# Weight tiles of group 0 prepared in three steps instead of two, and one product moved ahead on VectorE

## Chip, cores and metric

One core of a Trainium2 chip runs the whole kernel. The metric is the device time of one execution in microseconds; before, the median of three runs is 947.73 us (946.85 to 948.97).

## What is computed

A linear-attention layer (4 batches, 8 heads, 768 positions, 48 channels a head) is followed by two feed-forward layers of 3072 tokens, 384 model channels and 2048 inner channels.

```python
def _attn_ref(r, k, v, w, u):
    for t in range(S):
        kt, vt, rt = (k[:, :, t], v[:, :, t], r[:, :, t])
        cur = np.einsum('bhd,bhe->bhde', u[None] * kt, vt)
        y[:, :, t] = np.einsum('bhd,bhde->bhe', rt, state + cur)
        state = w[None, :, :, None] * state + np.einsum('bhd,bhe->bhde', kt, vt)

def _moe_ref(x, w_in, w_out):
    h = x @ w_in
    return (h * (1.0 / (1.0 + np.exp(-1.702 * h)))) @ w_out

def _moe2_ref(x, w_in, w_out):
    h = x @ w_in
    sp = np.where(h > 20.0, h, np.log1p(np.exp(np.minimum(h, 20.0))))
    return (h * np.tanh(sp)) @ w_out
```

The weights of both feed-forward layers come as 64-bit floating-point numbers.

## The kernel before, in words

**Tokens and blocks.** The 3072 tokens are 24 blocks of 128 (`j`), and six groups of 512 (`g`). Attention works block by block; for the first four blocks (j = 0 to 3, the tokens of group 0) it runs alone, lines 694 to 729. From then on (line 779) each of the 16 steps of a group, one for each tile of 128 inner channels (`m`), does the feed-forward work of one tile, and the attention of one further block is spread over four steps: its phases are `ph` 0 (`unit_a`, the products of queries and keys, and the mask), 1 (`unit_kv`, `unit_y`), 2 (`unit_x`, the additions to the state T, the next block's `products` and `powers`, its loads) and then `values`, `early_bonus` and `diagonal` for the next block. Block 4 starts one step late.

**Precision by split operands.** Each operand of a feed-forward product is split into a high part, rounded for TensorE, and a low part, the rest. A product takes three matmuls for each 128 rows: high x high, low x high, high x low (`PASSES`). `product_in` (line 596) makes `h` with nine matmuls of 512 columns, `product_out` (line 742) adds nine to the three accumulators `acc`. Step m issues `product_in` of tile m and, near its end, `product_out` of tile m - 1.

**A weight tile's way** (class `Layer`, lines 56 to 172). A tile holds the 768 columns that one step needs. `fetch(m)` (line 74) is five transfers on SP's queue into a raw buffer (`rawa`); tiles share three of these in turn, so a fetch waits until the tile three before has been read. `bits(m, 0)`, `bits(m, 1)`, `bits(m, 2)` are three DVE instructions over 128 x 768 (lines 123, 129, 132), which take the 32-bit pattern out of the 64-bit numbers into a pattern buffer (`wva`). `high(m)` is one ACT copy of the pattern to the rounded high part (line 155). `low(m, half)` subtracts high from pattern for 384 columns (line 163): half 0 on POOL, half 1 on DVE in group 0, and both on POOL for tiles 0 and 1.

**Order in group 0.** Nothing plans the order: each engine works through its instructions in the order of the code. `BARE_TILES` (line 35) tiles, 0 and 1, are prepared during the four bare blocks: `bits(0)` and its parts in j = 1, `bits(1)` and its parts in j = 2 (lines 711 to 724). In step m of group 0 (lines 796 to 803 and 820) come, in this order, the high part of tile m + 1 (ACT), its low part (POOL, DVE), the fetch of tile m + 4 (SP), and the first two pattern instructions of tile m + 2 (DVE), then gelu (line 804) and `gh` (line 805) on ACT, `gl` on DVE (line 806), the attention work of phases 0 or 2, and the third pattern instruction of tile m + 2. (Step 0 has no high, low or fetch, as tile 1 is ready.) So on DVE a step is low part, two pattern instructions, `gl`, attention, the third pattern instruction; on ACT it is high part, gelu, `gh`.

**Phase 2 on DVE** (lines 810 to 814): the split of x (`unit_x`, line 522: ACT copies `y` to `xha`, DVE subtracts for `xla`, line 528), two additions to T (line 520, or copies, line 518), and `products(j + 1)` (line 385, written to a tile `Am`), which the small matmuls `pa` of `early_bonus` (line 393) need; ACT then makes eight diagonal tiles from it (line 419). In group 0 `products` runs in steps 3, 6 and 10 (blocks 5, 6 and 7).

**Buffers.** The pattern buffer of a tile is `x2_1` for odd and `x2_3` for even m (lines 621 and 622); both names, as `x2_0` and `x2_2`, later hold results of the first layer, which are written from group 1 on. From group 1 on all sixteen weight tiles stay in SBUF, and steps prepare none.

Of the kernel before, what the change touches and what calls it, by code (L numbers as in the profile page):

```python
# [25 lines left out]
NF = 16  # L26
# [5 lines left out]
W_LO, W_HI = 0.8, 1.25  # L32
R2 = math.sqrt(0.5)
RAW = 3
BARE_TILES = 2
LAG = 4
NB = 2

# [557 lines left out]
def product_in(nc, lay, m, x, n, pool, name):  # L596
    h = pool.tile([P, 512], F32, tag="h", name=name)
    k = 0
    for kt in range(3):
        for wz, xz in PASSES:  # L600
            nc.tensor.matmul(h[:, :n], lhsT=lay.win(m, wz, kt), rhs=x[xz][:, kt, :], start=k == 0, stop=k == 8)  # L601
            k += 1
    return h


def feed_forward(tc, ctx, ins, out, w_sb, chk, consts, general):
# [4 lines left out]
    V, A = nc.vector, nc.scalar  # L611

    wpool = ctx.enter_context(tc.tile_pool(name="wpool", bufs=NF))
    spool = ctx.enter_context(tc.tile_pool(name="spool", bufs=2))
    xpool = ctx.enter_context(tc.tile_pool(name="xpool", bufs=2))
    x2pool = ctx.enter_context(tc.tile_pool(name="x2pool", bufs=1))
# [2 lines left out]
    late = {}  # L619

    l1 = Layer(nc, w1, wpool, lambda m: (x2pool, "x2_2", 1) if m % 3 == 2 else (spool, "raw", 2),
               lambda m: (x2pool, "x2_1" if m % 2 else "x2_3", 1, 768), "a", chk, spool, general, True)
    l2 = Layer(nc, w2, wpool, lambda m: (late["x"], "x2_5", 1) if m % 3 == 1 else (spool, "raw", 2),
               lambda m: (late["x"], "wv", 2, 768) if m % 4 > 1 else (late["b"], "sy"[m % 4], 2, NB * 512), "b", chk, spool, general)
    x2, xs, xs2 = {}, {}, {}
# [1 line left out]
    def new_x(g, tag):  # L627
        n = GROUPS[g]
        return (xpool.tile([P, 3, n], F32R, tag="xh", name=f"xh{tag}{g}"),
                xpool.tile([P, 3, n], F32R, tag="xl", name=f"xl{tag}{g}"))  # L630
# [20 lines left out]
    at = Attention(nc, apool, cpool, psum, chan, tok, general)  # L651

    def unit_x(j):
        t = j * C
        g = max(z for z in range(NG) if starts[z] <= t)
        if g not in xs:
            xs[g] = new_x(g, "a")
        at.unit_x(j, xs[g], t - starts[g])
# [27 lines left out]
    def parts(m):  # L686
        l1.high(m)
        l1.low(m, 0)
        l1.low(m, 1)
# [4 lines left out]
    for j in range(n_bare):  # L694

        more = j + 2 < n_bare
        at.unit_y(j, "acc", 3)
        if more:
            at.products(j + 2)
            at.powers(j + 2, V)  # L700
        if j + 1 == n_bare:
            unit_x(j)
        elif not general:
            for z in range(2):
                at.mask(j + 1, z)
        at.unit_t(j, 0, V)
        at.unit_t(j, 1, V)
        at.values(j + 1, G)
        if j + 1 < n_bare:
            at.unit_kv(j + 1, "y", 1)  # L710
        if j == 1:
            l1.bits(0)
        if j + 1 < n_bare:
            unit_x(j)
        if more:
            at.early_bonus(j + 2, "acc", 3)
            at.diagonal(j + 2, 0)
            at.diagonal(j + 2, 1)
            at.unit_a(j + 2)
        if j == 1:  # L720
            parts(0)
        if j == 2:
            l1.bits(1)
            parts(1)
        if general or j:
            at.load_rk(j + NRK)
        at.load_tok(j + 2)
        if j < 3:
            l1.fetch(j + 2)
# [12 lines left out]
    def product_out(g, m, gt):  # L742
        n = GROUPS[g]
        if m == 0:
            acc[g] = [psum.tile([P, 512], F32, tag="acc", name=f"acc{g}_{z}", bufs=3) for z in range(3)]
        for ct in range(3):
            for k, (wz, gz) in enumerate(PASSES):
                nc.tensor.matmul(acc[g][ct][:, :n], lhsT=l1.wout(m, wz, ct), rhs=gt[gz],  # L748
                                 start=m == 0 and k == 0, stop=m == NF - 1 and k == 2,
                                 skip_group_check=True)  # L750

    def evacuate(g):
        n = GROUPS[g]
        x2[g] = (x2pool if g < NG - 2 else late["x"]).tile([P, 3, n], F32, tag=f"x2_{g}", name=f"x2_{g}")
        for ct in range(3):
            if ct == 0 or g == NG - 1 or (ct == 1 and g == NG - 2):
                A.activation(out=x2[g][:, ct, :], in_=acc[g][ct][:, :n], func=AF.Copy)
            else:
                V.tensor_copy(out=x2[g][:, ct, :], in_=acc[g][ct][:, :n])
# [3 lines left out]
    def range_check(n):  # L763

        if n >= len(checks):
            return
        if n == 0:
            l1.check(0, 0)
            l1.check(1, 0)
        lay, m, part = checks[n]  # L770
        lay.check(m, part)
        if part == 1 and 0 < n < len(checks) - 2:
            lay, m, part = checks[n + 2]
            lay.check(m, 0)

    pend = None
    d = BARE_TILES
    checked = 0
    for g in range(NG - 1):
        n = GROUPS[g]  # L780
        for m in range(NF):

            j, q = n_bare + (g * NF + m) // 4, m % 4
            on = j < NJ

            ph = q - 1 if j == n_bare else q
            h = product_in(nc, l1, m, xs[g], n, hpool, f"h{g}_{m}")
            e = d - 1 if d > BARE_TILES else NF
            if on and ph == 0:
                at.unit_a(j)  # L790
            if on and ph == 1:
                at.unit_kv(j)
                at.unit_y(j)
            gh = gpool.tile([P, n], F32R, tag="gh", name=f"gh{g}_{m}")
            gl = gpool.tile([P, n], F32R, tag="gl", name=f"gl{g}_{m}", bufs=1 if general else 2)
            if g == 0:

                l1.high(e)
                l1.low(e, 0)
                l1.low(e, 1, V)  # L800
                l1.fetch(e + RAW)
                l1.bits(d, 0)
                l1.bits(d, 1)
            A.activation(out=h[:, :n], in_=h[:, :n], func=AF.Gelu_apprx_sigmoid)  # L804
            A.activation(out=gh, in_=h[:, :n], func=AF.Copy)  # L805
            V.tensor_tensor(out=gl, in0=h[:, :n], in1=gh.bitcast(F32), op=ALU.subtract)  # L806
            if on and ph == 0 and not general:
                for z in range(2):
                    at.mask(j, z)
            if on and ph == 2:  # L810
                unit_x(j)
                at.unit_t(j, 1, V)
                at.bonus(j + 1, 2, V)
                at.products(j + 1)

            for _ in range(0 if g == 0 else 2 if m % 8 == 7 else 1):
                range_check(checked)
                checked += 1
            if g == 0:
                l1.bits(d, 2)  # L820
                d += 1
            if on and ph == 0:
                at.bonus(j + 1, 0, G)
            if on and ph == 1:
                at.unit_t(j, 0, V if g == 0 else G)
                at.bonus(j + 1, 1, G)
            if on and ph == 2:
                at.load_rk(j + NRK)
                at.load_tok(j + 2)
                at.powers(j + 1, V if g == 0 else G)  # L830
            if on and q == 3:
                at.values(j + 1, G)
            if pend is not None:
                product_out(*pend)
                if pend[1] == NF - 1:
                    evacuate(pend[0])
            if on and (q == 3 or ph < 0):
                i = j if ph < 0 else j + 1
                at.early_bonus(i, "A", 2)
                at.diagonal(i, 0)  # L840
                at.diagonal(i, 1)
            pend = (g, m, (gh, gl))
# [220 lines left out]
```

## Time and profile before

| | |
|---|---|
| median of three runs | 947.73 us (946.85 to 948.97) |
| profiled execution | 946.47 us, of which the span is 944.6 us |
| PE busy | 908.9 us (96%) |
| DVE busy | 496.1 us (53%) |
| ACT busy | 570.9 us (60%) |
| POOL busy | 182.3 us (19%) |

The span runs from the first to the last instruction of the execution that was profiled. Engines: PE is TensorE, DVE VectorE, ACT ScalarE, POOL GpSimd, SP the engine that issues most transfers. A row of the time line gives the start, the length, engine, line and operation, output and inputs, their shapes and the count; in square brackets stands how long the engine had been idle and what ended that. A matmul's name lists one of its inputs: `h<-xha,wa` has the high part of x, `h<-xla,wa` the low one; `acc<-gh,wa` and `acc<-gl,wa` likewise. Numbers of buffers are left out, so every tile's pattern is called `wva`. PEclk is the granted TensorE clock as a share of 2.4 GHz.

### The profile page before, as it was taken

How to read it: one execution, taken by the hardware profiler on the slowest of the kernel's cores; microseconds unless marked ns; L12 is line 12 of the kernel's file. 1: busy time of each engine (PE TensorE's matmuls, PEld its weight loads, DVE VectorE, ACT ScalarE, POOL GpSimd, SP SyncE). 2: the span in 40 equal slices, each digit the busy share in tenths (PEclk: the TensorE clock that was granted, in tenths of full speed). 3: DMA queues.
4: the chain of work that ended last, by engine and by line, in shares of the span. 5: the costliest groups of instructions: out<-in, count | busy, mean ns of one | idle time of the engine just before them, and what ended most of it. 6: DMA issues, size and time to landing. Idle time of an engine off the chain costs nothing.

```text
span 944.6 us, 14242 instructions
## 1 busy us (share of the span) xinstructions
PE 908.9 (96%) x5766; PEld 770.2 (82%) x5766; DVE 496.1 (53%) x690; ACT 570.9 (60%) x896; POOL 182.3 (19%) x171
## 2 busy tenths in 40 slices
PE   6679999999999999999999889999999999999997
PEld 5567778887877878788888778999999999999986
DVE  7788873223223223322499556565555555555653
ACT  4344445546565555663355667677777777777773
POOL 3313353222432223320034012001010010010000
PEclk9799999999999999999999999999999999999999
DMA  9675633444344364431255000000000000000001
GB/s 203 162 185 151 177 109 109 143 136 156 112 142 143 112 182 121 135 122 35 70 197 200 2 1 1 1 33 1 34 1 1 34 1 1 34 1 1 34 1 37
DMA packets 34907, 78.42 MB, mean 83 GB/s; under 512 B 4368, under 2 KB 23568, under 8 KB 34832
## 3 DMA queue, kind: packets, MB, share of 16 engines
q1 hardware_dynamic: 33952, 77.09, 28.0%
q8 instruction: 47, 0.77, 0.4%
q10 hardware_dynamic: 880, 0.33, 0.2%
q14 instruction: 28, 0.23, 0.1%
HBM read 72.68 MB, written 4.72 MB: 82 GB/s over the span
## 4 chain that ended last, share of the span: by engine, by line
PE 78%; DVE 11%; issue 5%; DMA 3%; POOL 1%; ACT 1%; SPq 1%; ACTq 0%; DVEq 0%; POOLq 0%
PE bcc L591 20%; PE k L601 20%; PE acc L748 16%; PE h L601 14%; PE y L500 3%; PE A L443 2%; DVE wvb L132 2%; DVE wvb L129 2%; DVE wva L123 1%; DMA rkbuf<-in_chan_dram 1%; DVE wva L132 1%; PE kv L480 1%; DVE wb L163 1%; DVE wvb L123 1%; DVE gl L882 1%
## 5 line engine op out<-in xcount | busy, mean ns | idle before, releaser
L591 PE MATMUL bcc<-wb,bh 128*128 128x384 f32 x768 | 211.5, 337 | 0.0
L601 PE MATMUL h<-xha,wa 128*128 128x512 f32 x576 | 183.0, 398 | 3.6 <-POOL wa L163 2.7
L601 PE MATMUL k<-xhb,wb 128*128 128x512 f32 x576 | 180.8, 395 | 4.5 <-DVE y L554 2.6
L748 PE MATMUL acc<-gh,wa 128*128 128x512 f32 x576 | 184.7, 402 | 0.0
L806 DVE TENSOR_TENSOR gl<-h,gh 128x512 fp32r<-128x512 f32 x80 | 55.3, 691 | 228.9 <-ACT gh L805 228.2
L591 PEld LDWEIGHTS bcc<-wb,bh 128*128 128x128 f32 x768 | 140.4, 188 | 4.1
L804 ACT ACTIVATE h<-h 128x512 f32<-128x512 f32 x80 | 46.5, 581 | 144.7 <-PE h L601 141.9
L601 PEld LDWEIGHTS h<-xha,wa 128*128 128x128 f32 x576 | 109.8, 191 | 29.4 <-POOL wa L163 4.0
L591 PE MATMUL bcc<-wb,bl 128*128 128x384 f32 x384 | 129.1, 336 | 0.9 <-DVE bl L578 0.9
L748 PEld LDWEIGHTS acc<-gh,wa 128*128 128x128 f32 x576 | 105.0, 188 | 27.8 <-issue 3.2
L601 PEld LDWEIGHTS k<-xhb,wb 128*128 128x128 f32 x576 | 107.1, 189 | 24.1 <-DVE y L554 3.4
L554 DVE TENSOR_TENSOR y<-k,s 128x512 f32<-128x512 f32 x96 | 66.2, 692 | 94.0 <-ACT s L553 89.7
L601 PE MATMUL k<-xlb,wb 128*128 128x512 f32 x288 | 114.4, 397 | 0.0
L601 PE MATMUL h<-xla,wa 128*128 128x512 f32 x288 | 113.9, 396 | 0.0
L748 PE MATMUL acc<-gl,wa 128*128 128x512 f32 x288 | 113.7, 395 | 0.1
L565 DVE SCALAR_TENSOR_TENSOR y<-s,y 128x1024 f32<-128x1024 f32 x48 | 59.9, 1249 | 83.1 <-ACT s L564 83.1
L553 ACT ACTIVATE s<-k 128x512 f32<-128x512 f32 x96 | 57.4, 599 | 65.0 <-PE k L601 64.4
L591 PEld LDWEIGHTS bcc<-wb,bl 128*128 128x128 f32 x384 | 72.1, 188 | 5.5 <-DVE bl L578 1.6
L563 ACT ACTIVATE s<-s,one 128x1024 f32<-128x1024 f32 x48 | 55.4, 1154 | 34.1 <-DVE y L554 34.1
L642 POOL TENSOR_TENSOR xlb<-x,xhb 128x512 fp32r<-128x512 f32 x18 | 24.7, 1376 | 264.4 <-DVE xhb L641 258.8
L601 PEld LDWEIGHTS h<-xla,wa 128*128 128x128 f32 x288 | 55.2, 192 | 12.3 <-DVE xla L528 0.3
L748 PEld LDWEIGHTS acc<-gl,wa 128*128 128x128 f32 x288 | 54.1, 188 | 13.3 <-DVE gl L882 0.5
(119 smaller groups left out, 1180.2 us busy)
## 6 DMA issues: line engine op xcount, KB each, us to landing
chka<-in_w_dram SPq DMA_DIRECT2D x16, 768.0 KB, 4.5
chkb<-in_w_dram SPq DMA_DIRECT2D x16, 768.0 KB, 4.4
rawb<-in_w_dram SPq DMA_DIRECT2D x16, 768.0 KB, 4.3
tkv<-in_tok_dram SPq DMA_DIRECT2D x24, 384.0 KB, 5.9
rkbuf<-in_chan_dram SPq DMA_DIRECT2D x46, 192.0 KB, 5.1
rawa<-in_w_dram SPq DMA_DIRECT2D x48, 96.0 KB, 2.6
rawa<-in_w_dram SPq DMA_DIRECT2D x16, 288.0 KB, 3.6
out_dram<-o SPq DMA_DIRECT2D x10, 384.0 KB, 3.1
```

The lines of the kernel that those rows point to most:

```text
L132: V.scalar_tensor_tensor(out=v, in0=L, scalar=29, in1=v, op0=ALU.logical_shift_right, op1=ALU.bitwise_or)
L500: self.nc.tensor.matmul(y[32 * s:32 * s + rows, C * x:C * x + C], lhsT=lhsT, rhs=rhs, start=n == 0, stop=n == len(jobs[s]) - 1, skip_group ...
L553: nc.scalar.activation(out=self.s[:, z, :n], in_=h[:, :n], func=AF.Sigmoid)
L554: nc.vector.tensor_tensor(out=self.y[:, z, :n], in0=h[:, :n], in1=self.s[:, z, :n], op=ALU.mult)
L563: nc.scalar.activation(out=s, in_=s, func=AF.Arctan, scale=-1.0, bias=self.one)
L565: nc.vector.scalar_tensor_tensor(out=y, in0=s, scalar=R2, in1=y, op0=ALU.add, op1=ALU.mult)
L591: self.nc.tensor.matmul(self.acc[g][t][:, :DM], lhsT=gt[gz][:, t * P:t * P + P], rhs=self.lay.wout(m, wz), start=m == 0 and k == 0, stop=m ...
L601: nc.tensor.matmul(h[:, :n], lhsT=lay.win(m, wz, kt), rhs=x[xz][:, kt, :], start=k == 0, stop=k == 8)
L642: nc.gpsimd.tensor_tensor(out=xl[:, z, :], in0=x2[g][:, z, :], in1=xh[:, z, :].bitcast(F32), op=ALU.subtract)
L748: nc.tensor.matmul(acc[g][ct][:, :n], lhsT=l1.wout(m, wz, ct), rhs=gt[gz], start=m == 0 and k == 0, stop=m == NF - 1 and k == 2, skip_grou ...
L804: A.activation(out=h[:, :n], in_=h[:, :n], func=AF.Gelu_apprx_sigmoid)
L806: V.tensor_tensor(out=gl, in0=h[:, :n], in1=gh.bitcast(F32), op=ALU.subtract)
```

## The change

A third pattern buffer is taken (`x2_0`), and three tiles are begun ahead of group 0: tile 0 is ready, tile 1 has its high part from block j = 2 and gets both halves of its low part on POOL in j = 3, tile 2 gets its three pattern instructions in j = 3, ahead of that block's `unit_x`. In step m of group 0 the high part is now that of tile m + 2, the low part that of tile m + 1 (none in step 0), the fetch that of tile m + 5, and the pattern instructions those of tile m + 3. In phase 2 `products(j + 1)` is moved ahead of `unit_x` and the additions to T.

```diff
-BARE_TILES = 2
+BARE_TILES = 3
...
     l1 = Layer(nc, w1, wpool, lambda m: (x2pool, "x2_2", 1) if m % 3 == 2 else (spool, "raw", 2),
-               lambda m: (x2pool, "x2_1" if m % 2 else "x2_3", 1, 768), "a", chk, spool, general, True)
+               lambda m: (x2pool, ("x2_1", "x2_3", "x2_0")[m % 3], 1, 768), "a", chk, spool, general, True)
...
         if j + 1 == n_bare:
+            l1.low(1, 0)
+            l1.low(1, 1)
+            l1.bits(2)
             unit_x(j)
...
         if j == 2:
             l1.bits(1)
-            parts(1)
+            l1.high(1)
...
-            e = d - 1 if d > BARE_TILES else NF
...
             if g == 0:
 
-                l1.high(e)
-                l1.low(e, 0)
-                l1.low(e, 1, V)
-                l1.fetch(e + RAW)
+
+                l1.high(d - 1)
+                if m:
+                    l1.low(d - 2, 0)
+                    l1.low(d - 2, 1, V)
+                l1.fetch(d + RAW - 1)
                 l1.bits(d, 0)
                 l1.bits(d, 1)
...
             if on and ph == 2:
+                at.products(j + 1)
                 unit_x(j)
                 at.unit_t(j, 1, V)
                 at.bonus(j + 1, 2, V)
-                at.products(j + 1)
```

## Rows read from the trace of the kernel before

**Rows 1.** Busy time by stretch: PE, PEld, DVE, ACT, POOL; PEclk, DMA share, GB/s.

```profile
42.00:139.00 97.00, 88.38 (x626) 69.02 (x627) 83.20 (x106) 42.66 (x91) 33.28 (x29) 0.95 0.60 159
139.00:480.00 341.00, 341.00 (x2553) 273.59 (x2552) 108.35 (x182) 187.97 (x415) 89.32 (x84) 1.00 0.41 123
```

**Rows 2.** Waits of PE, 42 to 139 us: total us, times, longest us.

```profile
PE pa L393 <- DVE Am L385: 5.1, 2, 4.3
PE h L601 <- POOL wa L163: 2.7, 3, 1.5
...
PE kv L480 <- DVE Am L447: 0.5, 1, 0.5
```

**Rows 3.** Waits of all engines, 38 to 140 us.

```profile
DVE wa L163 <- ACT wa L155: 11.7, 12, 2.6
```

**Rows 4.** Time line of DVE, steps 2 and 3 of group 0.

```profile
54.98 0.95 DVE L132 SCALAR_TENSOR_TENSOR wva<-rawa,wva 128x768 int32<-128x768 int32 x1
56.84 0.56 DVE L163 TENSOR_TENSOR wa<-wva,wa 128x384 fp32r<-128x384 f32 x1 [0.91 <-ACT wa L155]
57.31 1.38 DVE L123 TENSOR_SCALAR wva<-rawa 128x768 int32<-128x768 int32 x1
...
59.60 0.69 DVE L806 TENSOR_TENSOR gl<-h,gh 128x512 fp32r<-128x512 f32 x1
60.20 0.95 DVE L132 SCALAR_TENSOR_TENSOR wva<-rawa,wva 128x768 int32<-128x768 int32 x1
...
62.07 0.56 DVE L163 TENSOR_TENSOR wa<-wva,wa 128x384 fp32r<-128x384 f32 x1 [0.45 <-ACT wa L155]
...
65.42 0.55 DVE L528 TENSOR_TENSOR xla<-y,xha 128x384 fp32r<-128x384 f32 x1
...
66.62 0.69 DVE L385 TENSOR_TENSOR Am<-rkbuf 112x512 f32<-112x512 f32 x1
```

**Rows 5.** Time line of ACT, step 2.

```profile
57.32 0.60 ACT L805 ACTIVATE gh<-h 128x512 fp32r<-128x512 f32 x1
```

**Rows 6.** Chain that ended last, end of group 0: start, us, work.

```profile
136.55 2.10 PE acc L748 x9
138.65 2.04 PE h L601 x9
```

**Rows 7.** Time line of PE, end of step 3 and first product of step 4.

```profile
67.46 1.02 PE L393 MATMUL pa<-ublk,Am 112*128 112x2 f32 x8 [4.26 <-DVE Am L385]
68.35 1.10 PE L601 MATMUL h<-xha,wa 128*128 128x512 f32 x2
...
72.17 1.16 PE L443 MATMUL A<-rkbuf 48*128 48x128 f32 x16
```

**Rows 8.** Time lines of DVE and POOL ahead of group 0.

```profile
38.27 0.96 DVE L132 SCALAR_TENSOR_TENSOR wva<-rawa,wva 128x768 int32<-128x768 int32 x1
41.90 0.56 DVE L528 TENSOR_TENSOR xla<-y,xha 128x384 fp32r<-128x384 f32 x1 [2.67 <-ACT xha L527]
...
40.18 1.95 POOL L163 TENSOR_TENSOR wa<-wva,wa 128x384 fp32r<-128x384 f32 x2 [2.76 <-ACT wa L155]
```

**Rows 9.** Time line of DVE, pattern instructions in step 0 and for tile 1.

```profile
36.60 1.63 DVE L129 SCALAR_TENSOR_TENSOR wva<-rawa,wva 128x768 int32<-128x768 int32 x1
...
46.35 0.55 DVE L123 TENSOR_SCALAR wva<-rawa 128x768 int32<-128x768 int32 x1
46.94 0.96 DVE L129 SCALAR_TENSOR_TENSOR wva<-rawa,wva 128x768 int32<-128x768 int32 x1
```

**Rows 10.** Time line of PE, first products of steps 8 and 12.

```profile
92.06 0.56 PE L601 MATMUL h<-xha,wa 128*128 128x512 f32 x1 [0.99 <-POOL wa L163]
...
95.54 1.26 PE L443 MATMUL A<-rkbuf 48*128 48x128 f32 x16
...
114.32 0.51 PE L601 MATMUL h<-xha,wa 128*128 128x512 f32 x1 [0.28 <-ACT wa L155]
116.37 0.79 PE L601 MATMUL h<-xha,wa 128*128 128x512 f32 x1 [1.55 <-POOL wa L163]
```

## The prediction

> **What bounds the kernel now.** I read the busy time of long stretches first [rows 1]. From 139 to 480 us TensorE is busy for all of its 341 us, so nothing done for another engine can help there. The stretch from 42 to 139 us is group 0 of the first layer: TensorE is busy 88.38 of 97 us, and its granted clock is 0.95 on the mean, so some products run at 1.2 instead of 2.4 GHz. The change touches group 0 and the 42 us ahead of it alone. What it saves there should reach the end undiminished, because TensorE works without a break behind it.
>
> Next, who lets TensorE wait in group 0 [rows 2]: the small bonus product `pa` waits 5.1 us for DVE's product of queries and keys (4.3 in one piece), and the first product `h` 2.7 us for POOL's part of a weight tile. In the list for all engines [rows 3] DVE's half of the low part waits 11.7 us, twelve times, for ACT's high part of the same tile.
>
> The time line of DVE in steps 2 and 3 shows why [rows 4]. DVE ends the last pattern instruction of a tile at 55.93 (54.98 + 0.95) and starts its half of that tile's low part only at 56.84: in these 0.91 us ACT makes the high part. From one third-pattern instruction (L132, 54.98) to the next (60.20) the loop takes 5.22 us. A step of TensorE, a product in and a product out, takes 2.04 + 2.10 = 4.14 us at full clock [rows 6]. So the loop through DVE and ACT, not TensorE, paces group 0, and TensorE pays where it catches up: for 4.26 us it has nothing until `pa` at 67.46, and the product behind it runs at 1.2 GHz [rows 7].
>
> **The change, part by part.** *Low part one step behind the high part.* In step m ACT now makes the high part of tile m+2, and POOL and DVE the low part of m+1, whose high part is a step old. No instruction is added to a step. DVE's wait goes: its loop becomes 5.22 - 0.91 = 4.31 us, an estimate that keeps every duration of rows 4. What is late next is `gl`, which needs ACT's `gh`: from 55.93 to the end of `gh` (57.32 + 0.60) it is 1.99 us [rows 5], and with `gl` (0.60 from its start to the next) and L132 (0.95) 3.54, less than 4.31. ACT's high part stays at the same place ahead of the gelu and waits for the same point of DVE, one tile on. Cost on ACT: nothing; if that cover were gone, a late pattern would hold the gelu back as it does now.
>
> *Fetches.* Each tile's five transfers still follow, on SP's queue, a pattern instruction three tiles earlier and lead their reader by the same number of steps; the `rk` and `tok` loads keep their places behind them. One fetch moves from step 1 to step 0. I cost them at nothing: in the list of waits no work on weights waits for a transfer. Were a lead too short, DVE would stop at L123.
>
> *Product behind `gl` (steps 3, 6 and 10).* In each of these steps the product passes the split of x and the two additions to T. In step 3 the product starts at 66.62, `xla` at 65.42 [rows 4], so it comes 1.20 us earlier. Those it passes start 0.6 us later; the split is read by group 1, the additions by a product three steps on, so this costs nothing unless their readers come up close behind.
>
> *Ahead of group 0.* Three pattern instructions for tile 2 now stand before the split of block 3, at a place where DVE idles from 39.23 to 41.90 [rows 8]. Alone they last 0.55 + 0.96 + 0.95 = 2.46 us (the first two as they run undisturbed in rows 9) and would fit; no delay is the lower end. But POOL makes its two halves of tile 1 there, 1.95 us from 40.18. The upper end: two held-up instructions, at 0.83 each (below), that is 39.23 + 2.46 + 1.66 = 43.35, or 1.4 us late. I take 0.9, beside the lower middle, since the first instruction ends before POOL starts. Step 1 gives the same 0.9 back by its own lost wait (one of the twelve), so the two cancel.
>
> *POOL beside DVE.* L123 takes 1.38 us with POOL's low part beside it [rows 4] and 0.55 alone [rows 9]: 0.83 us of DVE. The move lets POOL run a step earlier, so another instruction of DVE meets it. Bounds: a gain of 0.83 where it falls into a wait, a loss of 0.83 where it meets a second instruction. I take 0, as rows 4 hold one such meeting per step already. The Trainium skill, GPSIMD Engine Reference, section Specifications, speaks against the change here: POOL's SBUF interfaces are shared with VectorE, with contention for instructions in a 2-port mode or with two SBUF inputs. By that rule L129, L132 and the low part are all exposed, and a second meeting per step (14 x 0.83 = 11.6 us) would cost more than the sum below gives; the trace agrees as far as L123 and, at 1.63 us [rows 9], L129 go.
>
> **The sum.**
> - Step 3: `pa` starts earlier by 0.91 (step 2's wait) + 0.45 (step 3's own, the wait before 62.07 in rows 4) + 1.20 (order) = 2.56 us.
> - Step 4: the product at 1.2 GHz takes 72.17 - 68.35 = 3.82 instead of 2.04 us [rows 7, 6]. With the pause cut to about 1.7 us I take full clock: 1.78. If the clock still falls, 0.
> - Step 8: a pause of 0.99 for POOL's low part, and eight matmuls in 95.54 - 92.06 = 3.48 instead of 8/9 of 2.04 = 1.81 [rows 10]: 2.66.
> - Step 12: pauses of 0.28 and 1.55, and the eight matmuls behind them as in step 8, 1.67 [rows 10]: 3.50.
> - Step 15: a pause of 0.17, the third of rows 2's waits for POOL.
>
> Together 10.7 us. Against it stands that DVE's new loop (4.31) is still a little longer than TensorE's step (4.14): over the twelve steps in which patterns are made, 12 x 0.17 = 2.0 us of new short waits. Between nothing (waits filled by attention products) and 4 (attention work on DVE adds as much again) I take 2.0. Net 8.7 us. The profiled execution took 946.47 us (span 944.6 and 1.9 around it), hence 937.8; it lies 1.26 below the median of the runs shown (947.73), so I forecast **939.0**.
>
> **Rivals.**
> *DVE stays the pace (0.17).* POOL meets a second instruction of DVE in half of the 14 steps: 7 x 0.83 = 5.8 us, leaving 2.9: 944.8. For it: DVE is busy 83.20 of 97 us [rows 1]. Against: POOL's low parts are short, and DVE has instructions that read PSUM between.
>
> *The wait only moves (0.07).* DVE reaches `gl` 0.9 us sooner and waits there for `gh`, and the weights are late as before: 947.7. For it: ACT's chain is untouched. Against: the 3.54 us worked out above, and that the low part's inputs are a whole step old.
>
> *TensorE's clock falls more often (0.11), slower than before.* Today three products run at 1.2 GHz, each behind a pause of 1 to 4 us. If the long pauses become short ones in every step, the clock may stay low over several products, at 1.78 us each (3.82 against 2.04). The place is steps 1 to 12. From five products at 1.2 GHz beyond those cleared, the 8.7 us are used up; eight cost 14.2, giving 947.7 - 8.7 + 14.2 = 953.2. Against it: with 8.6 us of pauses the clock of group 0 was still 0.95 on the mean [rows 1], and the pause that I leave in, 0.5 us for the mask [rows 2], is shorter than any ahead of a slow product. The Trainium skill, TensorE: Matmul & The Clock Gate, section "A second HAM failure mode: psum-queue depth-cycling", says that frequent micro-idles between groups of matmuls make the clock oscillate; the trace shows that only behind the longer pauses.
>
> **How the numbers follow.** The forecast has 0.65, and 935.5 to 941.5 alone; its low end is with no new waits and a little more won of what there is: pauses of 5.1 + 2.7 + 0.5 + 0.3 = 8.6 us [rows 2, 10] and slow products of 1.78 + 2 x 1.67 = 5.1 are 13.7 together, which would give 934.0. The range 934.5 to 945.0 takes in most of the first rival and leaves out about 2 in 10. A measurement of this kernel can tell 0.2% (1.9 us) from no change. Faster by more: 0.65 + 0.17 = 0.82; within: 0.07; slower: 0.11.
>
> **What would show it.** Right: DVE's low part waits for ACT near 0 instead of 11.7 us; no wait of `h` for POOL; `pa`'s long wait under 2.5 us; the clock of 42 to 130 us at 0.98 or more; TensorE without a pause from about 130 us on, and all later stretches as long as before. Wrong: `gl` waiting for `gh`, L129 at 1.6 us throughout (first rival), a granted clock below 0.95 in group 0 (third), DVE stopped at L123 for a transfer, or the split of block 3 starting over 2 us later than 41.90.

## Result and profile after

The changed kernel takes **934.73 us** (median of four runs, 934.06 to 935.54) against 947.29 for the kernel before beside it: ratio 0.9874, 95% interval 0.9849 to 0.9898, 12.6 us faster. The forecast was 939.0, and the range began at 934.5. A second measurement of the same kernel, in a later group of runs, gave 936.17 us and a ratio of 0.9895 (0.9877 to 0.9913), 9.6 us. The gain is 10 to 13 us; the forecast of 8.7 was somewhat small, and two of the four runs of the first measurement lie just below the range. Two profiles of the changed kernel were taken, the first of a run of 934.06 us, the second, with the later group, of one of 936.45.

Busy time by stretch, the changed kernel, first profile (columns as in [rows 1]); group 0 now runs from 39.5 to 127.3 us:

```profile
42.00:128.00 86.00, 85.39 (x624) 68.54 (x623) 76.19 (x102) 42.18 (x90) 33.36 (x29) 0.95 0.68 176
128.00:467.00 339.00, 339.00 (x2544) 271.92 (x2543) 106.56 (x181) 186.58 (x413) 88.16 (x83) 1.00 0.40 124
```

TensorE is busy for all but 0.6 of 86 us, where it was idle for 8.6 of 97. The window begins just behind a pause of 0.78 us inside the first product, to which the section on the start of group 0 comes back. The list of waits of all engines (38 to 130 us) says who waits instead, the changed kernel first, then the kernel before (38 to 140 us):

```profile
...
ACT wa L155 <- DVE wva L132: 28.0, 11, 3.9
ACT h L808 <- PE h L601: 15.8, 9, 3.6
DVE gl L810 <- ACT gh L809: 9.0, 8, 2.8
...
PE h L601 <- DVE xla L528: 0.8, 1, 0.8
PE pa L393 <- DVE Am L385: 0.6, 1, 0.6
...
PE h L601 <- ACT xha L527: 0.6, 1, 0.6
```

```profile
...
ACT wa L155 <- DVE wva L132: 46.5, 14, 4.9
...
ACT h L804 <- PE h L601: 2.5, 2, 2.2
...
DVE gl L806 <- ACT gh L805: 0.2, 1, 0.2
```

The wait of DVE's low part for ACT (11.7 us in [rows 3]) and those of `h` for POOL (2.7 in [rows 2]) are gone. DVE now waits for ACT's `gh` (9.0 us, 0.2 before), and ACT's gelu for TensorE's `h` (15.8, 2.5 before): behind step 3, where TensorE waits for nothing, the pace has passed to TensorE. ACT's waits for a pattern of DVE have become fewer (28.0 us, 46.5 before). The time line of DVE in steps 2 and 3, to be held against [rows 4], and the two turns of L132 that enclose the next step without attention work:

```profile
57.63 0.94 DVE L132 SCALAR_TENSOR_TENSOR wva<-rawa,wva 128x768 int32<-128x768 int32 x1
58.49 0.55 DVE L510 TENSOR_TENSOR T<-T,wp 112x384 f32<-112x384 f32 x1
58.96 0.55 DVE L163 TENSOR_TENSOR wa<-wva,wa 128x384 fp32r<-128x384 f32 x1
59.43 0.55 DVE L123 TENSOR_SCALAR wva<-rawa 128x768 int32<-128x768 int32 x1
60.02 1.65 DVE L129 SCALAR_TENSOR_TENSOR wva<-rawa,wva 128x768 int32<-128x768 int32 x1
63.47 0.69 DVE L810 TENSOR_TENSOR gl<-h,gh 128x512 fp32r<-128x512 f32 x1 [1.80 <-ACT gh L809]
64.08 0.68 DVE L385 TENSOR_TENSOR Am<-rkbuf 112x512 f32<-112x512 f32 x1
64.68 0.55 DVE L528 TENSOR_TENSOR xla<-y,xha 128x384 fp32r<-128x384 f32 x1
...
72.35 0.94 DVE L132 SCALAR_TENSOR_TENSOR wva<-rawa,wva 128x768 int32<-128x768 int32 x1
...
76.60 0.94 DVE L132 SCALAR_TENSOR_TENSOR wva<-rawa,wva 128x768 int32<-128x768 int32 x1
```

The low part (L163) follows at once, POOL's half now holds up L129 (1.65 us) instead of L123 (0.55), and DVE has 1.80 us to spare ahead of `gl`. That spare time is of this profile: in the second one DVE waits for nothing from 42 to 67 us, so there it sets the time up to the product of step 3. From one L132 to the next (72.35 to 76.60) a step without attention takes DVE 4.25 us.

Where the time went, by six marks from the time line of TensorE (starts, us):

| | before | changed | changed, second profile |
|---|---|---|---|
| first product `h` | 41.92 | 39.49 | 40.75 |
| `h` of step 2 | 51.67 | 53.48 | 52.59 |
| `pa` of step 3 | 67.46 | 64.91 | 64.64 |
| scores `A` of step 4 | 72.17 | 68.08 | 68.61 |
| scores `A` in step 0 of group 1 | 140.63 | 129.48 | 130.71 |
| end of the span | 944.6 | 932.3 | 934.6 |

Up to the `pa` of step 3 the change wins 2.55 us (2.82 in the second profile), from there to the scores of step 4 1.54 (0.74), in the next twelve steps 7.06 (6.36), and behind group 0 1.15 (0.08): 12.30 (10.00).

### The profile page after: what moved, and what is told of

Same layout as the page of the kernel before. It is cut to its first block, busy times and chain, and to the rows that moved or that the text cites. A ratio compares the mean times of both kernels' runs of the same rounds, so it can differ in the third digit from the quotient of the medians.

```text
span 932.3 us, 14246 instructions
## 1 busy us (share of the span) xinstructions
PE 905.4 (97%) x5766; PEld 768.8 (82%) x5766; DVE 493.3 (53%) x690; ACT 570.9 (61%) x896; POOL 182.0 (20%) x171
## 4 chain that ended last, share of the span: by engine, by line
PE 86%; DVE 8%; issue 2%; DMA 2%; ACT 0%; POOL 0%; ACTq 0%; POOLq 0%; DVEq 0%; SPq 0%
PE bcc L591 21%; PE k L601 20%; PE acc L751 19%; PE h L601 18%; PE y L500 4%; PE A L443 3%; DVE wvb L132 2%; DVE wvb L129 2%; DMA tkv<-in_tok_dram 1%; PE kv L480 1%; PE pa L393 1%; DVE wb L163 1%; DVE wvb L123 1%; DVE gl L886 1%; DVE bl L578 1%
## 5 line engine op out<-in xcount | busy, mean ns | idle before, releaser
L808 ACT ACTIVATE h<-h 128x512 f32<-128x512 f32 x80 | 46.5, 581 | 154.6 <-PE h L601 154.6
```

## Experiments

A profile shows one execution. Where its time lies away from the median, it is given beside what is read from it.

### Which half of the change does it: the order, or the three steps

Before, with the order alone (`order_only`):

```diff
             if on and ph == 2:
+                at.products(j + 1)
                 unit_x(j)
                 at.unit_t(j, 1, V)
                 at.bonus(j + 1, 2, V)
-                at.products(j + 1)
```

> The kernel before with products(j + 1) moved ahead of the split of x, and nothing else. My theory (the order is worth what it moves at step 3): the bonus product pa of step 3 starts 1.2 us earlier, its pause goes from 4.26 to about 3.1 us, and the product behind it stays at 1.2 GHz: 946.1 us, 1.2 less than before. With that product back at full clock 1.8 more: 944.3. Rival (the order, not the three steps, is the larger part of the 12.6 us): 940 or less.

Measured: 944.48 us, ratio 0.9983 (0.9969 to 0.9996), 1.9 us of gain beside 946.40. The time line of TensorE, from an execution of 947.18 us, the longest of the eleven:

```profile
67.30 1.84 PE L393 MATMUL pa<-ublk,Am 112*128 112x2 f32 x8 [3.03 <-DVE Am L385]
69.00 1.20 PE L601 MATMUL h<-xha,wa 128*128 128x512 f32 x2
```

The pause went from 4.26 to 3.03 us, as theory had it (3.1), and in this execution the product behind it stayed slow. The median gain lies between that forecast for a slow product (1.2 us) and that for one at full clock (3.0). The complement, the three steps without the order (`steps_only`), is the changed kernel with the same five lines the other way round:

> The changed kernel with products(j + 1) back behind the split of x and the additions to T: the three-step tiles alone. My theory: the pause ahead of pa in step 3 grows from 0.61 to about 1.8 us and the rest stays: 935.9 us, and 937.7 if the product behind that pause falls to 1.2 GHz. Rival (the order carries most): 942 or more.

Measured: 938.75 us, ratio 0.9927 (0.9910 to 0.9944), 7.7 us. In the profiled execution (941.0 us) the pause ahead of `pa` was 1.81 us, as expected, and the product behind it fell to 1.2 GHz (69.86 to the scores at 73.69, 3.83 us). So the three steps are the larger part. With them the order is worth 2.6 to 4.0 us against the two measurements of the changed kernel, alone 1.9; the intervals do not tell these apart, and 7.7 and 1.9 add up to the 9.6 of the second measurement. That the order with the three steps also saves a product from the lower clock is seen in the first profile, but not shown for the medians.

### Is it DVE's wait, or the late weight tiles

`wait_back` makes the low part of the tile whose high part was just made. All tiles are ready a step ahead, but DVE and POOL wait for ACT again:

```diff
                 l1.high(d - 1)
-                if m:
-                    l1.low(d - 2, 0)
-                    l1.low(d - 2, 1, V)
+                l1.low(d - 1, 0)
+                l1.low(d - 1, 1, V)
```

> The changed kernel, but each step makes the low part of the tile whose high part it has just made (m + 2), one step earlier than in the change: DVE waits for ACT again, and yet every weight tile is ready a step ahead. Theory A (the wait of DVE on ACT sets the pace, a loop of 5.2 us): DVE's low part waits about 0.9 us in most steps again, pa in step 3 pauses 2 us or more, and the time is 939 to 944 us. Theory B (it was the late weight tiles and the slow products behind them that cost): no pause of h, and 934 to 936 us, as the changed kernel.

Measured: 946.09 us, ratio 0.9988 (0.9971 to 1.0004): nothing is left of the gain that is clear of noise. DVE's waits (38 to 128 us), then its time line in step 2:

```profile
DVE wa L163 <- ACT wa L155: 10.0, 10, 2.2
```

```profile
57.09 0.94 DVE L132 SCALAR_TENSOR_TENSOR wva<-rawa,wva 128x768 int32<-128x768 int32 x1
58.94 0.56 DVE L163 TENSOR_TENSOR wa<-wva,wa 128x384 fp32r<-128x384 f32 x1 [0.91 <-ACT wa L155]
...
62.30 0.95 DVE L132 SCALAR_TENSOR_TENSOR wva<-rawa,wva 128x768 int32<-128x768 int32 x1
```

The loop is 5.21 us again (5.22 in [rows 4]), and `h` never waits for POOL. TensorE loses the time elsewhere: 3.0 us at `pa` and 1.1 at `kv` for DVE's products and mask, 1.0 at `acc` for `gl`, and 4.0 more at `kv` that the list puts down to no engine. The time lines show whose these are: both times `kv` starts 0.81 us after DVE started its mask (125.70 and 126.51 in the longer one), much as in the wait that the list does name (0.76). That decides for theory A, though with more loss than it said (946 instead of 939 to 944): the length of DVE's loop costs the time, and the late weight tiles were only one of the places where it showed.

The run brings back one thing more. POOL's half meets L123 again, and the three pattern instructions take 3.34 us a step on the mean, as before (3.35), instead of 3.02. In the step shown this hardly counts: 5.21 us less the wait of 0.91 is 4.30, against 4.25 in the changed kernel. Over the group it is some 4 us of DVE beside 10.0 us of waits. The next run takes POOL out of it.

### POOL beside DVE

`low_dve` takes the low part off POOL in group 0:

```diff
-                    l1.low(d - 2, 0)
+                    l1.low(d - 2, 0, V)
                     l1.low(d - 2, 1, V)
```

> The changed kernel with both halves of the low part on DVE in group 0, so that POOL makes none there. Theory A (POOL's half holds up one instruction of DVE with two SBUF inputs by 0.85 us, now L129): L129 takes 0.96 us in every step without other POOL work, a step of DVE is 0.85 - 0.47 = 0.4 us shorter than with POOL's help, and the time is within 1 us of the changed kernel, 935 to 937 us, since TensorE is the bound there. Theory B (L129 is long for another reason, such as transfers into the buffers that it reads): L129 stays near 1.5 us on the mean, and DVE's step grows by 0.47 us: 937 to 940 us.

Measured: 934.64 us, ratio 0.9887 (0.9869 to 0.9905), the same as the changed kernel. The lines of the pattern instructions (L123, L129, L132) of DVE in groups by line (busy us, mean ns), first the kernel before (42 to 139 us), then the changed kernel and `low_dve` (42 to 128 us):

```profile
L123 DVE TENSOR_SCALAR wva<-rawa 128x768 int32<-128x768 int32 x14 | 16.7, 1194 | 0.0
L129 DVE SCALAR_TENSOR_TENSOR wva<-rawa,wva 128x768 int32<-128x768 int32 x14 | 16.2, 1155 | 0.5
L132 DVE SCALAR_TENSOR_TENSOR wva<-rawa,wva 128x768 int32<-128x768 int32 x14 | 14.0, 997 | 0.0
```

```profile
L129 DVE SCALAR_TENSOR_TENSOR wva<-rawa,wva 128x768 int32<-128x768 int32 x13 | 19.6, 1511 | 0.4
L132 DVE SCALAR_TENSOR_TENSOR wva<-rawa,wva 128x768 int32<-128x768 int32 x13 | 12.4, 953 | 0.1
...
L123 DVE TENSOR_SCALAR wva<-rawa 128x768 int32<-128x768 int32 x13 | 7.2, 551 | 0.0
```

```profile
L129 DVE SCALAR_TENSOR_TENSOR wva<-rawa,wva 128x768 int32<-128x768 int32 x13 | 13.2, 1013 | 0.5
L132 DVE SCALAR_TENSOR_TENSOR wva<-rawa,wva 128x768 int32<-128x768 int32 x13 | 13.0, 1000 | 0.1
...
L123 DVE TENSOR_SCALAR wva<-rawa 128x768 int32<-128x768 int32 x13 | 7.2, 553 | 0.0
```

L129 falls from 1511 to 1013 ns on the mean, so POOL's half was what held it up; theory B falls. A step of DVE without attention takes 3.87 us there (L132 at 70.78 and 74.65) against 4.25 (72.35 and 76.60) in the changed kernel, and the time does not follow: behind step 3 DVE no longer sets it.

### The start of group 0

The changed kernel once more (`after_again`), as a base for the next three:

> The changed kernel once more, beside the next three on the same chip. If the 2.4 us by which its first product started earlier than in the kernel before (39.5 against 41.9 us) is chance of the transfers in the first 30 us, a new profile starts it between 41 and 43 us, and the time is 934 to 937 us. If it belongs to the change, it starts at about 39.5 us again. The stretch from the first product to that of step 2 shows again whether TensorE's clock falls there: about 14 us if it does, about 10 if not.

Measured: 936.17 us. The first product started at 40.75, between the two marks. In `steps_only`, `wait_back`, `low_dve` and `prod_first`, whose code is the same up to there, it started between 40.13 and 42.50. So the 2.4 us by which the first profile was ahead can be chance. Busy time from the first product to that of step 2, first profile, then second, then the kernel before (the last three figures are granted clock, DMA share, GB/s):

```profile
39.40:53.40 14.00, 13.13 (x51) 10.10 (x52) 13.03 (x18) 6.60 (x16) 7.11 (x6) 0.62 0.86 198
```

```profile
40.70:52.50 11.80, 10.13 (x51) 7.90 (x52) 11.55 (x15) 6.47 (x15) 6.65 (x6) 0.86 0.88 216
```

```profile
41.90:51.60 9.70, 8.85 (x51) 6.78 (x52) 8.61 (x12) 5.74 (x14) 2.54 (x4) 1.00 0.76 188
```

In both profiles of the changed kernel TensorE stops inside its first product for the split of block 3:

```profile
41.49 0.80 PE L601 MATMUL h<-xla,wa 128*128 128x512 f32 x1 [0.78 <-DVE xla L528]
```

```profile
43.10 0.79 PE L601 MATMUL h<-xla,wa 128*128 128x512 f32 x1 [1.62 <-DVE xla L528]
```

Two ways to free that split were tried. `start_free` moves tile 2's patterns behind the powers of block 4:

```diff
-            l1.bits(2)
             unit_x(j)
...
     at.powers(n_bare, V)
+    l1.bits(2)
...
-                l1.high(d - 1)
                 if m:
+                    l1.high(d - 1)
...
             A.activation(out=gh, in_=h[:, :n], func=AF.Copy)
+            if g == 0 and m == 0:
+                l1.high(2)
```

> The changed kernel with the three pattern instructions of tile 2 behind the powers of block 4 and its high part behind gh of step 0: nothing stands ahead of the split of block 3 any more. Theory A (the 0.8 us pause for that split holds TensorE at 1.2 GHz for the first two products and pa): the first product starts and runs as in the kernel before, the first two products take about 2.1 us each at full clock, and the time is 930 to 932 us. Theory B (the clock at that point has nothing to do with the split): the pause of 0.8 us goes, the products stay at 1.2 GHz: 934 us; with gl of step 0 2.5 us later it may lose up to 2 us: 937.

Measured: 935.73 us, ratio 0.9881 (0.9861 to 0.9901). `early_bits` moves tile 1's patterns ahead of the mask of block 3, where DVE idles, and tile 2's to the place that tile 1's had; these three still stand ahead of the split, as tile 1's did in the kernel before:

```diff
         elif not general:
+            if j == 2:
+                l1.bits(1)
             for z in range(2):
                 at.mask(j + 1, z)
...
-            l1.bits(2)
             unit_x(j)
...
         if j == 2:
-            l1.bits(1)
+            if general:
+                l1.bits(1)
+            l1.bits(2)
             l1.high(1)
```

> The changed kernel with the pattern instructions of tile 1 moved ahead of the mask of block 3, where DVE idles about 2 us, and those of tile 2 in their former place: nothing stands ahead of the split of block 3, and nothing is late in step 0. Theory A (the split held up by tile 2's patterns is what holds TensorE's clock down at the start): from the first product to that of step 2 it takes 10.5 us or less, pa of step 3 pauses 0.6 us or less, and the time is 3 to 4 us below the changed kernel of this batch, 931 us. Theory B (the clock at that point is set by what TensorE does before): 13 us or more in that stretch, and the time of the changed kernel within 1 us.

Measured: 934.35 us, ratio 0.9873 (0.9857 to 0.9889). Both profiles show at the start what theory A said: no pause for the split, clock 1.00, and 10.48 and 9.36 us to step 2. The times that it gave (930 to 932 and 931 us) did not come: they hardly moved, 0.4 us (in another group of runs) and 1.8 us below `after_again`. In the profiles most of what was won was lost again by step 4. The time lines of DVE in step 2 and of TensorE in steps 3 and 4 of `early_bits`, from an execution of 935.72 us, the longest of the five:

```profile
56.09 0.72 DVE L123 TENSOR_SCALAR wva<-rawa 128x768 int32<-128x768 int32 x1 [1.20 <-DMA rawa<-in_w_dram]
```

```profile
63.71 1.25 PE L393 MATMUL pa<-ublk,Am 112*128 112x2 f32 x8 [1.72 <-DVE Am L385]
64.83 1.20 PE L601 MATMUL h<-xha,wa 128*128 128x512 f32 x2
...
68.43 1.16 PE L443 MATMUL A<-rkbuf 48*128 48x128 f32 x16
```

Step 2 starts 1.43 us earlier than in `after_again` (51.16 against 52.59), `pa` 0.93 and the scores of step 4 only 0.18: in this execution the earlier start turned into a wait of DVE for the transfer of a raw tile, a pause of 1.72 us and a product mostly at 1.2 GHz (3.60 us).

The lists of DVE's waits say why a faster start of TensorE brings little. From 42 to 67 us they are empty in `after_again`, `extra_mm`, `early_extra`, `prod_first` and `all_three`, and that of `start_free` has 0.2 us: up to the product of step 3 DVE has nothing to spare, so TensorE, when it starts faster, waits longer for that product. Where TensorE was slowest at the start, DVE did wait: 2.6 us in the first profile (clock 0.62) and 2.7 in `steps_only` (0.61).

Nine matmuls that nobody reads, ahead of `unit_kv` of block 3 in the changed kernel (`extra_mm`):

```diff
+        if j == 2 and not general:
+            extra = hpool.tile([P, 512], F32, tag="h", name="extra")
+            for k in range(9):
+                nc.tensor.matmul(extra[:, :256], lhsT=l1.win(0, 0, k % 3), rhs=xs[0][0][:, k % 3, :256], start=k == 0, stop=k == 8)
         if j + 1 < n_bare:
             at.unit_kv(j + 1, "y", 1)
```

> The changed kernel with nine matmuls of 256 columns, whose result nobody reads, ahead of unit_kv of block 3, where TensorE waits about 2 us for POOL. They keep TensorE busy and change nothing on DVE. Theory A (the held-up split alone does it): the clock still falls at the first products, stretch to step 2 about 14 us, time of the changed kernel within 1 us. Theory B (the clock there follows what TensorE did in the few us before): the granted clock of the first two products is 1.00, the stretch takes 11 us or less, and the time is 2 to 4 us lower.

Measured: 936.04 us, as `after_again` (936.17); the clock from the first product to step 2 was 0.86 and the stretch 12.0 us, as there (0.86 and 11.8). Neither theory's figure was met exactly. The extra work did nothing for the time; for the clock one profile says little, since it was 0.61 to 0.86 in the six profiles that have the same start without the extra work. Both together (`early_extra`):

> Both at once: pattern instructions of tile 1 ahead of the mask of block 3, and the nine matmuls. If the two causes are separate, the time is the lowest of the four, 929 to 931 us; if one alone is the cause, it is that of the better of the two within 1 us.

Measured: 934.76 us, ratio 0.9875 (0.9859 to 0.9892): that of `early_bits`. What decides the clock at the start stays open. With tile 2's patterns directly ahead of the split it was below 1.00 in all seven profiles; with them elsewhere it was 1.00 in four of five. But the pause for the split is not what does it. Of the two profiles of the changed kernel the one with the longer pauses (1.43 and 1.62 against 0.59 and 0.78 us) had the higher clock, and these four (the last two kernels follow below) go against it:

| | pause for the split, us | clock, first product to step 2 |
|---|---|---|
| `wait_back` | none | 0.79 |
| `prod_early` | none | 0.80 |
| `early_extra` | 0.66 | 1.00 |
| `all_three` | 1.58 | 1.00 |

### What is left in step 3

`prod_first` puts `products(j + 1)` ahead of `gl`:

```diff
+            if on and ph == 2:
+                at.products(j + 1)
             A.activation(out=h[:, :n], in_=h[:, :n], func=AF.Gelu_apprx_sigmoid)
...
             if on and ph == 2:
-                at.products(j + 1)
                 unit_x(j)
```

> The changed kernel with products(j + 1) one place further ahead: directly ahead of gl, where DVE idles 1.8 us in step 3 for gh. Theory A (what is left of the pause in step 3 is the chain h, gelu, gh, gl, product, pa): no pause ahead of pa, the first product of step 4 always at full clock (2.3 us up to the scores), and 1.5 to 2.7 us less than the changed kernel: 933.5 to 934.5 us. Theory B (DVE is simply full up to step 3): the pause stays at 0.6 to 1.2 us and the time at 936.

Measured: 934.93 us, ratio 0.9880 (0.9859 to 0.9902), 1.2 us below `after_again`, in another group of runs, and within its interval. A pause of 0.49 us was left, with full clock behind it, and DVE waits for nothing up to there. So neither theory came with its figures, and DVE being full (theory B) is part of what is left. With the patterns moved as in `early_bits` as well (`prod_early`):

> The product directly ahead of gl and, as in early_bits, the pattern instructions of tile 1 ahead of the mask of block 3. Alone, the earlier start was lost again in a longer pause ahead of pa in step 3 (1.7 us). Theory A (that pause is gone once the product does not hang behind gl): the earlier start of 2 to 3 us is kept, 931 to 933 us. Theory B (DVE is full up to step 3): as prod_first within 1 us.

Measured: 933.07 us, ratio 0.9860 (0.9837 to 0.9883), 1.9 us below `prod_first`, which the intervals do not tell apart. Its time line of TensorE has no pause ahead of `pa`:

```profile
63.05 1.02 PE L393 MATMUL pa<-ublk,Am 112*128 112x2 f32 x8
63.94 0.71 PE L601 MATMUL h<-xha,wa 128*128 128x512 f32 x2
...
66.83 1.16 PE L443 MATMUL A<-rkbuf 48*128 48x128 f32 x16 [0.57 <-ACT Am L419]
```

The product keeps full clock, and the next wait is one that `prod_first` has too (0.60 us), 0.57 us for ACT's diagonal tiles. `all_three` adds a move on POOL ahead of group 0:

```diff
         at.values(j + 1, G)
+        if j == 2:
+            l1.low(0, 0)
+            l1.low(0, 1)
...
         if j == 1:
-            parts(0)
+            l1.high(0)
```

> prod_early, and ahead of group 0 the low part of tile 0 behind the values of block 3 on POOL, because unit_kv of block 3 waits about 2 us for those values behind it. If that wait is on the path, the first product of group 0 starts 1.5 to 2 us earlier and the time is 929 to 932 us; if the block waits for its transfer anyway, it is that of prod_early within 1 us.

Measured: 931.27 us (930.74 to 934.22), ratio 0.9859 (0.9837 to 0.9882). The wait of `unit_kv` of block 3 for POOL (1.94 us in `prod_early`) is gone from its time line, and the first product starts at 38.97, earlier than in any other profile; as such starts vary by 3 us without a change of code, the one does not prove the other. It is the lowest median of the study, some 3 to 5 us below the changed kernel. By its interval it can't be told from `prod_early`, nor for certain from the changed kernel.

## Why the prediction was right, and where it was not

The mechanism was the one forecast. The size was near, with one term wrong and some chance in the rest: 934.73 us lies 0.2 us above the low end of the range and outside the 935.5 to 941.5 us of the main case, the second measurement (936.17) inside both. Against the 8.7 us, the first profile won 3.6 more: 2.0 that were not lost to new waits, 0.7 in the twelve steps, 1.15 behind group 0 (0.08 in the second profile, and no part of the forecast), less 0.2 in step 4.

**DVE's wait: right.** It went from 11.7 us to none; the loop became 4.25 us where 4.31 had been estimated. `wait_back` shows that the gain goes when the wait comes back, though late tiles do not come back with it. Of the signs named for it these came: no wait of `h` for POOL, `pa`'s wait under 2.5 us, TensorE without a pause later on. One failed: the clock of 42 to 130 us is 0.95 (0.96 in the second profile), with its slow products at the start. Two signs of being wrong came as well, `gl` waiting for `gh` and L129 at 1.5 us on the mean; neither cost time, for the reasons below.

**The new short waits, 2.0 us: the step that failed.** I set DVE's new loop (4.31) against a bare step of TensorE (4.14) and left out that TensorE does attention work in these steps too. The twelve steps between the scores of step 4 and those of group 1 take it 61.40 us, 5.1 each, and not one wait for DVE is in the list behind step 4; it is DVE that waits for `gh`, 9.0 us over the whole group, 2.6 of them ahead of step 4. So the 2.0 us were not lost.

**Steps 8, 12 and 15: right.** 6.33 us predicted; the twelve steps became 7.06 shorter, 6.36 in the second profile.

**Step 3 and the order: right in sum, by luck in part.** 2.56 us predicted, 2.55 measured at `pa`. But the sum let the start and step 1 cancel. In truth the first profile came to its first product 2.43 us sooner, then lost 4.24 us up to step 2, and won 4.36 from there to `pa`. The second profile has 1.17, 2.09 and 3.74 us for these, 2.82 in sum. As the 2.43 us can be chance, the agreement to 0.01 us is luck. That the sum is near all the same has a reason: up to the product of step 3 DVE has nothing to spare, and what TensorE wins or loses at the start ends in the pause ahead of `pa`.

**Step 4: too large, in one profile of two.** 1.78 us predicted for full clock; 1.54 measured with a pause of 0.61 us, 0.74 with one of 1.22, where part of the product ran slow.

**Fetches: nothing, as costed.** DVE never stopped for a transfer in either profile of the changed kernel; it did once, for 1.20 us, in `early_bits`, whose start is faster.

**Ahead of group 0: under-priced.** I took the split 0.9 us late, with 1.4 as the upper end. In the first profile `xha` starts at 38.95 and `xla` at 40.89; with the distance of the kernel before (0.52 us) it would be 39.47, so it came 1.42 late, the upper end. In the second profile the same sum (40.23, 42.51) gives 1.76, beyond it. POOL's two halves hit the last pattern instruction, which took 1.65 us.

**POOL beside DVE: 0 taken, a little won.** L123 fell from 1194 to 551 ns, L129 rose from 1155 to 1511; one meeting per step, only with another instruction. With L132 the three take 3.02 us a step instead of 3.35 (3.13 in the second profile). Against it the powers of the next block (L373, five times in the group) rose from 1226 to 1617 ns. The section Specifications of the Trainium skill's GPSIMD Engine Reference was borne out so far that L129, with two SBUF inputs, is held up (1.65 us beside POOL, 0.96 without); a second meeting per step, which would have brought the first rival, did not come.

**Rivals.** DVE stayed the pace up to the product of step 3, but not behind it. The wait that only moves was seen in form (`gl` waits for `gh`), but ACT waited for TensorE in turn, so it costs nothing. The clock did fall, though in steps 0 and 1 instead of all over group 0. That the pause of step 3 hid most of its price is argued from the small gain of `start_free` and `early_bits`, not shown by itself. The oscillation under frequent micro-idles that the Trainium skill describes (TensorE: Matmul & The Clock Gate, section "A second HAM failure mode: psum-queue depth-cycling") could not be tried here: from step 5 on there are none.

## What to carry to other kernels

Where two in-order engines hand each other a tile within one step, add up the loop from an instruction to its next turn; if it is longer than the bound engine's step, put a step between the two halves rather than making either faster. Then look for what the earlier engine does next before shortening anything else: here 2.5 us won by TensorE at the start were worth little, because DVE had nothing to spare up to the product that both meet at in step 3. And when a loop is weighed against the bound engine, count all the work of that engine in the step, not only the main products.

## What the runs showed of the hardware

The clock of the product behind `pa` of step 3 went with the pause ahead of it: with none and with 0.49, 0.61 and 1.08 us it ran at full clock, with 1.22 us partly slow, and with 1.15, 1.43, 1.72, 1.81, 3.03 and 4.26 us all or most of it at 1.2 GHz, 3.6 to 4.1 us instead of 2.3 up to the scores. Between 1.08 and 1.22 us the length of the pause alone did not decide it. A POOL subtraction of 384 columns held up DVE's L123 before and L129 after by some 0.7 to 0.85 us, whichever stood beside it. DVE does the same subtraction itself in 0.47 us (its two halves take 1.02 us in `low_dve`, one 0.55), so POOL's help cost DVE more than it saved: a step of DVE without it took 3.87 instead of 4.25 us. Nine extra matmuls in a wait ahead of the start did not change the time.
